# Fused transposes for the near strided blocks, a new opening order, and other units for the attention stages of two groups

## The chip, the cores and the metric

The kernel runs on one core of a Trainium2 chip. The metric is device time in microseconds (us), lower is better, as the median of several executions. One further execution is recorded by the hardware profiler; all trace times below are microseconds from the start of its span.

## The reference

Attention over 4 batches, 8 heads, 576 positions of 64 values. Heads 0 to 3 are local (a query sees the 32 positions up to itself), heads 4 to 7 strided (a query sees earlier positions with the same residue modulo 32). Its output feeds two feed-forward blocks.

```python
scores = np.where(masks, scale * q @ k.T, -1e9)
attn = exp(scores - max) / (sum + 1e-9);  x = attn @ v      # 2304 rows of 512
h = x @ w_in;  x = (h - tanh(h)) @ w_out                    # 512 -> 2048 -> 512
xn = x / rms(x) * rms_g
out = (silu(xn @ w_gate) * (xn @ w_val)) @ w_out2           # 512 -> 1536 -> 512
```

## The kernel before

The 2304 rows are cut into nine **blocks** of 256, numbered 0 to 8, and these into five **groups**: (0,1), (2,3), (4), (5,6), (7,8). The attention of a block gives one half of the tile `xs` (local heads) and the other half (strided heads). For each group the first feed-forward block runs over 16 **units** f: `pe_h` (12 matmuls into `ps_h`), tanh on ACT (L675), `dve_g` (`tg`, L680), a split into a high part on ACT (`g`, L686) and a low part on DVE (L691), and `pe_x` (12 or 24 matmuls into `ps_x`), which runs one or two units late. Every fp32 operand is split in two parts, hence three matmuls for each product. After group 4 the second feed-forward block follows, untouched by the change. A matmul of any kind has line 143, the helper `mm`.

**Attention in stages.** Blocks 0 to 3 are the near ones. A block's local heads (class `Local`, letter L) and, where the block is one run of positions, its strided heads (class `Dense`, letter D) go through stages with one letter each: `s` scores on PE into two PSUM banks; `m` row maximum on DVE (L289, or L292 for later blocks); `e` exponential on ACT (L303); `n` normalisation on DVE (`sm`, L313); `p` transposes on PE into a bank `ps_p` (L322); `c` copy to `pT` on ACT (L326); `v` the product with v on PE into `ps_v`; `y` the high part of the result on ACT (L329) and `z` its low part on DVE (L333), both into `xs`. Stages m, e, n, p, c, y, z each exist twice, for half 0 and half 1 (64 queries of two sub-blocks each). For a near D block a half is `sm` of 128 x 64 for each of four heads; `p` makes four transposes of 64 columns into 64 partitions for each half, and `v` contracts over 64 partitions.

**The opening.** Up to the third unit the order on all engines is written out by hand, in the text `START`. A word is a stage, a block, a kind, a half and a bank: `p0L1m0` is p of block 0, local, half 1, bank m0. `A`, `B`, `P`, `Q` with a number convert weight tile 0, 1, ... (scale on ACT, L162; merge on DVE, L168 and L169; high part on ACT, L176; low part on DVE, L180); `h`, `T`, `G`, `I`, `J`, `X` are the steps of the first three units. Each engine works through its own instructions in the order in which `START` names them. The loads are issued ahead of it, by the first line of `START`: table, q and k of blocks 0, v, then weights and block 1.

**After the opening** the stages of the next group's attention are spread over the units of the running group. `STINT` lists, for running groups 1, 2 and 3, the units f after whose `pe_h` a whole stage is put (a stage `s` carries m, e, n with it, `p` carries c, `v` carries y and z):

```python
def pe_work():
    if g in STINT:
        wk.run_pe(len(wk.pe) if f in STINT[g] else 0)
```

In group 2 the list works through v of block 5, then block 6: s, p of L, s of D, v of L, p, v of D. In group 3 it is s, p, v of block 7 and then of block 8. From group 1 on PE keeps program order; the other engines are ordered by a scheduler. Blocks 4, 5, 7 and 8 have their strided heads done without PE: GpSimd (POOL) multiplies (L495 for scores, L528 for values), DVE sums (L500, L535). Their v comes through the buffer `sv` (L476), which block 3's D uses before them, so that this load waits for v of block 3.

Of the kernel before, what the change touches and what calls it, by code (L numbers as in the profile page):

```python
# [7 lines left out]
F32 = mybir.dt.float32  # L8
# [14 lines left out]

START = """
<tabcdwABwCDwww2ww
W9 s0Lx m0L1 s0Dx e0L1 m0L0 e0L0 n0L1 p0L1m0 m0D0 m0D1 n0L0 e0D0 n0D0 c0L1a A0 p0L0h1 e0D1 p0D0m0 c0L0a s1Lx c0D0a
B0 s1Dx n0D1 P0 A1 m1L0 Q0 p0D1h0 v0Lm0 m1D0 e1L0 c0D1a y0L1 B1 y0L0 n1L0 v0Dh0 z0L0 m1L1 z0L1 e1D0 m1D1 y0D1 z0D1
y0D0 z0D0 e1L1 P1 p1L0m0 A2 e1D1 n1L1 h0h1 p1L1m1 c1L0a Q1 B2 n1D0 c1L1a h1h0 T0 P2 p1D0m0 T1 c1D0a n1D1 p1D1m1 G0
c1D1a v1Lh1 Q2 I0 G1 I1 y1L1 y1L0 v1Dm1 y1D1 y1D0 J0 J1 z1L1 A3 A4 z1L0 z1D1 z1D0 X0 B3 P3 B4 h2h1 T2 G2 I2 Q3 J2
"""  # L30


# [1 line left out]
def attn_moe_moe_kernel(  # L34
# [24 lines left out]
    nc = tc.nc  # L59
    B, _, NC, D = q_str.shape  # L60
# [41 lines left out]
    ps_h = ctx.enter_context(tc.tile_pool(name="ps_h", bufs=1, space=PSUM))  # L102
    ps_m = ctx.enter_context(tc.tile_pool(name="ps_m", bufs=1, space=PSUM))
# [11 lines left out]
    ident, mask, dmask = tab[:, 192:320], tab[:, 320:416], tab[:, 416:544]  # L115
# [128 lines left out]
    class Heads:  # L244
        def __init__(self, j):
            self.j, self.near, self.early = j, j < NEAR, j < EA
            self.ps, self.sm, self.nm, self.ss, self.pp, self.pT, self.v = {}, {}, {}, {}, {}, {}, {}
            self.slot = {}

        def room(self, name, i, words):  # L250

# [28 lines left out]
        def st_m(self, i):  # L280

            w, ps = self.w, self.ps
            self.sm[i] = sm = self.room("sm", i, 4 * w).rearrange("q (h p t) -> q h p t", h=2, p=2)
            self.nm[i] = nm = att.tile([128, 2, 2], F32, tag="nm", name="nm", bufs=4)
            self.ss[i] = att.tile([128, 2, 2], F32, tag="ss", name="ss", bufs=4)
            m = dmask if w == 128 else mask if not self.near else add[96][:, i] if w == 96 else add[64]
            for hh in range(2):
                if self.early:
                    nc.vector.tensor_reduce(out=nm[:, hh], in_=ps[hh][:, i], axis=AX.X, op=ALU.max)  # L289
                else:  # L290
                    for p in range(2):
# [23 lines left out]
            )  # L315

        def st_p(self, i, bank):
            self.pp[i] = ps = bank("ps_p")[0:self.w].rearrange("k (h p t) -> k h p t", h=2, p=2)
            sm = self.sm.pop(i)
            for hh in range(2):  # L320
                for p in range(2):
                    nc.tensor.transpose(ps[:, hh, p, :], sm[:, hh, p, :], ident)  # L322

        def st_c(self, i, copy):
            self.pT[i] = pT = self.room("pT", i, 512)[0:self.w].rearrange("k (h p t) -> k h p t", h=2, p=2)
            copy(out=pT, in_=self.pp.pop(i))  # L326

        def st_y(self, i):
# [10 lines left out]
    class Local(Heads):  # L339
        w = 96  # L340
# [73 lines left out]
    class Dense(Heads):  # L414
        def __init__(self, j, b, t0):
            super().__init__(j)
            self.b, self.w = b, 128 if t0 else 64
            self.at = [self.w * u for u in range(4)]

        def load_qk(self):  # L420
            w = self.w
# [11 lines left out]

        def load_v(self):
            t = wts.tile([128, 1024], F32, tag="w", name="dv") if self.early else one.tile([128, NC * D], F32, tag="sv", name="dv")
            t = t[0:self.w, :1024]
            self.v = t.rearrange("k (g f) -> k g f", g=4)
            nc.sync.dma_start(out=t, in_=(v_near if self.near else v_far)[self.b])

        def st_v(self, bank):  # L440
            ps = bank("ps_v").rearrange("r (i n g t) -> r i n g t", i=2, n=2, g=2)
            for i in range(2):
                pT = self.pT.pop(i)
                for g in range(2):
# [143 lines left out]
    class Work:  # L588
# [22 lines left out]
        @staticmethod  # L611
        def stage(o, nm):
            if nm == "s":
                o.st_s(bank_m)
                for i in range(2):
                    o.st_m(i)
                    o.st_e(i)
                for i in range(2):
                    o.st_n(i)
            elif nm == "p":  # L620
                for i in range(2):
                    o.st_p(i, bank_m)
                    o.st_c(i, nc.scalar.copy)
            else:
                o.st_v(bank_m)
                for i in range(2):
                    o.st_o(i)
            nxt = o.nxt
            if nxt:
                if nm == "s":  # L630
                    nxt.load_qk()
                if nm == "v" and isinstance(o, Local):
                    for i in range(2):
                        nxt.load_v(i)
                elif nm == "v":
                    nxt.load_v()
# [206 lines left out]
    xq, first_units, pg = [], units[:3], None  # L843
    del units[:3]

    def bank_of(tag):
        if tag == "x":
            return bank_x
        return lambda name: {"h": ps_h, "m": ps_m}[tag[0]].tile([128, 512], F32, tag=tag, name=name)

    def first(word):

        op, rest = word[0], word[1:]
        if op == "<":
            for c in rest:
                loads[c]()
        elif op == "W":
            z = att.tile([128, 512], F32, tag="sm", name="zero").bitcast(BF16)[:, :512]
            nc.vector.memset(z, 0.0)
            ps = bank_of("m0")("ps_w")  # L860
            for _ in range(int(rest)):
                mm(ps, z[:, :128], z, True, True)
        elif op in "ABPQ":
            w = st1.ws[int(rest)]
            pool, tag, e = st1.place(int(rest))
            if op == "A":
                w.scale()
            elif op == "B":
                w.merge()
                st1.i = int(rest) + 1  # L870
            elif op == "P":
                w.high(pool, tag)
            else:
                w.low(e)
        elif op == "h":
            pe_h(*first_units[int(rest[0])], bank_of(rest[1:]))
        elif op in "TGIJX":
            u = first_units[int(rest)]
            {"T": act_tanh, "G": dve_g, "I": g_hi, "J": g_lo, "X": pe_x}[op](*u)
            if op == "J":  # L880
                xq.append(u)
            if op == "X":
                xq.remove(u)
        else:
            j, kind, rest = int(rest[0]), rest[1], rest[2:]
            o = loc[j] if kind == "L" else strd[j][0]
            fn = getattr(o, "st_" + op)
            if op in "sv":
                fn(bank_of(rest))
            elif op == "p":  # L890
                fn(int(rest[0]), bank_of(rest[1:]))
            elif op == "c":
                fn(int(rest[0]), nc.scalar.copy)
            else:
                fn(int(rest))

# [98 lines left out]
def lay_out(inputs):  # L995
# [50 lines left out]
    def flat(*parts):  # L1046
        return _np.concatenate([a.reshape(*a.shape[:2], -1) for a in parts], axis=2)
# [5 lines left out]
    laid = dict(  # L1053
        near_l=flat(q_l[:, :, :8], k_l[:, :, :, :256]),
        near_v=flat(*(v_l[:, a:a + 96] for a in (0, 32, 96, 160))),
        near_d=flat(q_d[:, 0], keys(8)), v_near=values(8).reshape(B, 64, 1024),
        q_loc=q_l, k_loc=k_l, v_loc=v_l,
        q_str=lanes(q), k_str=lanes(k), v_str=lanes(v),
        q_far=q_d[:, 1], k_far=keys(16).reshape(B, 128, 1024), v_far=values(16).reshape(B, 128, 1024),
# [27 lines left out]
```

## Time and profile before

| | us |
|---|---|
| median of 3 runs | 929.55 (925.61 to 930.08) |
| the profiled execution, its own time | 927.72 |
| its span, first to last instruction | 925.9 |
| PE busy | 906.0 (98%) |
| DVE busy | 533.8 (58%) |
| ACT busy | 343.4 (37%) |
| POOL busy | 154.3 (17%) |

PE is the matmul engine, DVE VectorE, ACT ScalarE, POOL GpSimd, SP the queue that issues the loads. The span is nearly all PE time, so what matters is where PE stands still or runs at its lower clock, and what it is then waiting for.

### The profile page before, as it was taken

How to read it: one execution, taken by the hardware profiler on the slowest of the kernel's cores; microseconds unless marked ns; L12 is line 12 of the kernel's file. 1: busy time of each engine (PE TensorE's matmuls, PEld its weight loads, DVE VectorE, ACT ScalarE, POOL GpSimd, SP SyncE). 2: the span in 40 equal slices, each digit the busy share in tenths (PEclk: the TensorE clock that was granted, in tenths of full speed). 3: DMA queues.
4: the chain of work that ended last, by engine and by line, in shares of the span. 5: the costliest groups of instructions: out<-in, count | busy, mean ns of one | idle time of the engine just before them, and what ended most of it. 6: DMA issues, size and time to landing. Idle time of an engine off the chain costs nothing.

```text
span 925.9 us, 13596 instructions
## 1 busy us (share of the span) xinstructions
PE 906.0 (98%) x5251; PEld 754.7 (82%) x5251; DVE 533.8 (58%) x1195; ACT 343.4 (37%) x800; POOL 154.3 (17%) x211
## 2 busy tenths in 40 slices
PE   6999999998999999999999999999999999999998
PEld 4888878887898788888888888888888888888897
DVE  5899968986779886289996361272126212411221
ACT  5878633233443333366584131131122212211111
POOL 0000347782366852000000000000000000000000
PEclk8899999999999999999999999999999999999999
DMA  9946224220313100175462010110010001000100
GB/s 279 355 178 223 77 80 145 72 95 1 111 52 105 41 1 1 66 266 191 160 227 92 1 46 0 46 46 1 1 45 1 23 1 45 1 1 1 46 1 23
DMA packets 33729, 72.86 MB, mean 79 GB/s; under 512 B 6976, under 2 KB 15552, under 8 KB 33664
## 3 DMA queue, kind: packets, MB, share of 16 engines
q1 hardware_dynamic: 33664, 71.99, 23.3%
q8 instruction: 41, 0.67, 0.3%
q14 instruction: 24, 0.20, 0.1%
HBM read 62.54 MB, written 9.44 MB: 78 GB/s over the span
## 4 chain that ended last, share of the span: by engine, by line
PE 69%; DVE 5%; POOL 2%; ACT 1%; issue 0%; ACTq 0%; POOLq 0%; DVEq 0%
PE ps_x L143 26%; PE ps_h L143 26%; PE ps_m L143 16%; DVE so L535 3%; POOL pr L495 2%; DVE tg L680 1%; DVE g L691 0%; POOL pr L528 0%; PE ps_p L322 0%; ACT sm L303 0%; DVE sm L292 0%; PE ps_v L143 0%; DVE sm L313 0%; DVE xs L333 0%; DVE pr L543 0%
## 5 line engine op out<-in xcount | busy, mean ns | idle before, releaser
L143 PE MATMUL ps_h<-xs,w 128*128 128x512 f32 (+1 forms) x984 | 216.2, 369 | 3.9 <-DVE tg L680 3.9
L143 PE MATMUL ps_x<-g,w 128*128 128x512 f32 (+1 forms) x984 | 215.9, 368 | 0.0
L143 PEld LDWEIGHTS ps_h<-xs,w 128*128 128x128 f32 x984 | 171.1, 191 | 34.4 <-DVE tg L680 4.8
L143 PEld LDWEIGHTS ps_x<-g,w 128*128 128x128 f32 x984 | 169.5, 190 | 30.7 <-issue 0.2
L790 DVE SCALAR_TENSOR_TENSOR s<-ps_m,s 128x512 f32<-128x512 f32 (+1 forms) x60 | 38.3, 638 | 239.5 <-PE ps_m L143 239.5
L143 PE MATMUL ps_h<-xn,w 128*128 128x512 f32 (+1 forms) x720 | 158.9, 369 | 0.0
L143 PE MATMUL ps_m<-xn,w 128*128 128x512 f32 (+1 forms) x720 | 158.1, 368 | 0.0
L143 PE MATMUL ps_x<-w,p 128*128 128x512 f32 x648 | 157.8, 391 | 0.0
L143 PEld LDWEIGHTS ps_h<-xn,w 128*128 128x128 f32 x720 | 126.8, 188 | 24.4
L143 PEld LDWEIGHTS ps_m<-xn,w 128*128 128x128 f32 x720 | 125.9, 188 | 23.1
L143 PEld LDWEIGHTS ps_x<-w,p 128*128 128x128 f32 x648 | 120.7, 188 | 25.6
L495 POOL TENSOR_TENSOR pr<-sk,sq 128x256 f32<-128x256 f32 (+2 forms) x101 | 83.5, 862 | 132.7 <-DMA sk<-in_k_str_dram 107.3
L789 ACT ACTIVATE s<-ps_h 128x512 f32<-128x512 f32 (+1 forms) x60 | 33.4, 556 | 176.3 <-PE ps_h L143 176.1
L792 ACT CAST p<-s 128x512 fp32r<-128x512 f32 (+1 forms) x60 | 34.7, 578 | 128.7 <-DVE s L790 128.7
L528 POOL TENSOR_TENSOR pr<-sv,se 128x288 f32<-128x288 f32 (+12 forms) x104 | 70.4, 698 | 68.0 <-DVE so L535 19.6
L686 ACT CAST g<-tg 128x512 fp32r<-128x512 f32 (+1 forms) x82 | 46.4, 567 | 83.4 <-DVE tg L680 83.4
L675 ACT ACTIVATE tg<-ps_h 128x512 f32<-128x512 f32 (+1 forms) x82 | 44.4, 542 | 70.2 <-PE ps_h L143 70.0
L680 DVE SCALAR_TENSOR_TENSOR tg<-ps_h,tg 128x512 f32<-128x512 f32 (+1 forms) x82 | 50.7, 618 | 31.9 <-ACT tg L675 31.7
L535 DVE TENSOR_REDUCE so<-pr 128x16 f32<-128x272 f32 (+11 forms) x104 | 65.0, 650 | 5.3 <-POOL pr L528 5.0
L691 DVE TENSOR_TENSOR g<-tg,g 128x512 fp32r<-128x512 f32 (+1 forms) x82 | 56.3, 687 | 13.4 <-ACT g L686 12.8
L793 DVE TENSOR_TENSOR p<-s,p 128x512 fp32r<-128x512 f32 (+1 forms) x60 | 38.3, 638 | 27.5 <-ACT p L792 27.2
L162 ACT ACTIVATE ca<-raw 128x512 f32<-128x512 f32 x68 | 45.7, 673 | 19.4 <-DMA raw<-in_w_val_dram 7.1
(77 smaller groups left out, 621.4 us busy)
## 6 DMA issues: line engine op xcount, KB each, us to landing
raw<-in_w_out_dram SPq DMA_DIRECT2D x28, 512.0 KB, 5.1
raw<-in_w_in_dram SPq DMA_DIRECT2D x16, 512.0 KB, 8.5
raw<-in_w_gate_dram SPq DMA_DIRECT2D x12, 512.0 KB, 4.4
raw<-in_w_val_dram SPq DMA_DIRECT2D x12, 512.0 KB, 4.1
x2d<-xe SPq DMA_DIRECT2D x36, 128.0 KB, 1.8
x<-x2d SPq DMA_DIRECT2D x16, 256.0 KB, 4.3
out_dram<-o SPq DMA_DIRECT2D x16, 256.0 KB, 2.0
sk<-in_k_str_dram SPq DMA_DIRECT2D x4, 576.0 KB, 3.7
```

The costliest lines, as they stand in the source:

```text
L143: nc.tensor.matmul(out_, lhsT, rhs, start=start, stop=stop, skip_group_check=True)
L162: nc.scalar.activation(out=self.a, in_=hi.bitcast(F32), func=ACTF.Prelu, scale=2.0 ** -111, alpha=-(2.0 ** 32))
L495: nc.gpsimd.tensor_tensor(out=pr, in0=self.k[:, a:e, :], in1=self.q[:, c - c0:c - c0 + 1, :].to_broadcast([128, e - a, D]), op=ALU.mult,)
L528: nc.gpsimd.tensor_tensor(out=pr, in0=self.v[:, 0:c + 1, a:e], in1=self.e[:, c - c0, 0:c + 1].unsqueeze(2).to_broadcast([128, c + 1, e - a ...
L535: pend.append(lambda: nc.vector.tensor_reduce(out=o[:, c - g0, a:e], in_=pr.rearrange("l c d -> l d c"), axis=AX.X, op=ALU.add))
L675: nc.scalar.activation(out=t, in_=h_of[g, f, a], func=ACTF.Tanh, scale=WS)
L680: nc.vector.scalar_tensor_tensor(out=t, in0=h_of.pop((g, f, a)), scalar=WS, in1=t, op0=ALU.mult, op1=ALU.subtract)
L686: nc.scalar.copy(out=t[:, 0], in_=t_of[g, f, a])
L691: nc.vector.tensor_tensor(out=t[:, 1], in0=t_of.pop((g, f, a)), in1=t[:, 0].bitcast(F32), op=ALU.subtract)
L790: nc.vector.scalar_tensor_tensor(out=s, in0=r[1], scalar=WS, in1=s, op0=ALU.mult, op1=ALU.mult)
L792: nc.scalar.copy(out=t[:, 0], in_=s)
L793: nc.vector.tensor_tensor(out=t[:, 1], in0=s, in1=t[:, 0].bitcast(F32), op=ALU.subtract)
```

## The change

1. Near D blocks 0 to 3 (`fused`): both halves' `sm` lie side by side in one tile (half as the second last index), `p` makes four transposes of 128 columns instead of eight of 64, `c` one copy of 128 partitions instead of two of 64. `v` (`st_v2`) reads half i from partitions 64i to 64i+63 of `pT` and of v, which is laid out and loaded as 128 x 512 instead of 64 x 1024 (the same bytes), and writes the halves to two banks instead of one; the number of matmuls stays 32.
2. `START` is another text: same steps, another order.
3. `STINT`: in group 2 the first two stages stand after units 1 and 3 instead of 2 and 3; in group 3 the six stand after 1, 4, 6, 8, 11, 13 instead of 1, 3, 5, 8, 10, 12.

```diff
-W9 s0Lx m0L1 s0Dx e0L1 m0L0 e0L0 n0L1 p0L1m0 m0D0 m0D1 n0L0 e0D0 n0D0 c0L1a A0 p0L0h1 e0D1 p0D0m0 c0L0a s1Lx c0D0a
...
+W9 s0Lx m0L0 e0L0 m0L1 s0Dx n0L0 e0L1 m0D0 p0L0m1 m0D1 s1Lx A0 e0D0 B0 c0L0a n0L1 p0L1h1 P0 Q0 m1L0 m1L1 e0D1 c0L1a
+v0Lh0 s1Dx n0D1 n0D0 A1 e1L0 p0Dh1 e1L1 y0L1 n1L0 m1D0 m1D1 c0Da n1L1 v0Dm0m1 y0L0 e1D0 y0D1 z0L0 y0D0 z0L1 p1L0h1
...
-    STINT = {1: (4, 6, 8, 11, 14), 2: (2, 3, 6, 7, 9, 10, 13), 3: (1, 3, 5, 8, 10, 12)}
+    STINT = {1: (4, 6, 8, 11, 14), 2: (1, 3, 6, 7, 9, 10, 13), 3: (1, 4, 6, 8, 11, 13)}
...
         def st_p(self, i, bank):
-            self.pp[i] = ps = bank("ps_p")[0:self.w].rearrange("k (h p t) -> k h p t", h=2, p=2)
+            n = 2 * self.w if self.fused else self.w
+            self.pp[i] = ps = bank("ps_p")[0:n].rearrange("k (h p t) -> k h p t", h=2, p=2)
             sm = self.sm.pop(i)
             for hh in range(2):
                 for p in range(2):
-                    nc.tensor.transpose(ps[:, hh, p, :], sm[:, hh, p, :], ident)
+                    x = self.both[:, hh, p].rearrange("q i t -> q (i t)") if self.fused else sm[:, hh, p, :]
+                    nc.tensor.transpose(ps[:, hh, p, :], x, ident)
...
+        def st_v2(self, bank):
+            ps = [bank("ps_v")[:, :256].rearrange("r (n g t) -> r n g t", n=2, g=2) for _ in range(2)]
+            pT = self.pT.pop(0)
+            for g in range(2):
+                for n in range(2):
+                    for h in range(4):
+                        for i in range(2):
+                            a, r = 64 * h + 32 * n, slice(64 * i, 64 * i + 64)
+                            mm(
+                                ps[i][32 * h:32 * h + 32, n, g], self.v[r, g, a:a + 32],
+                                pT[r, h % 2, h // 2, 64 * g:64 * g + 64], True, True,
+                            )
```

How the instructions stand, at three places. ACT in the opening, before; `ca` is the scaling of a weight that has just been loaded (`raw_112` the first, `raw_118` the second), `sm` 128x64 the exponentials of D of block 0, `pT` the copies:

```order
L303 ACTIVATE sm_223,ss_225<-ps_s_182,nm_224 128x64 x2
L303 ACTIVATE sm_223,ss_225<-ps_s_183,nm_224 128x64 x2
L326 COPY pT_244<-ps_p_218 96x512
L162 ACTIVATE ca_246<-raw_112 128x512
L303 ACTIVATE sm_223,ss_230<-ps_s_182,nm_229 128x64 x2
L303 ACTIVATE sm_223,ss_230<-ps_s_183,nm_229 128x64 x2
L326 COPY pT_244<-ps_p_248 96x512
L326 COPY pT_283<-ps_p_257 64x512
L176 CAST w_311<-ct_285 128x512
L162 ACTIVATE ca_313<-raw_118 128x512
```

The same stretch of ACT in the change:

```order
L162 ACTIVATE ca_254<-raw_112 128x512
L310 ACTIVATE sm_218,ss_220<-ps_s_191,nm_219 128x64 x2
L310 ACTIVATE sm_218,ss_220<-ps_s_192,nm_219 128x64 x2
L336 COPY pT_263<-ps_p_224 96x512
L176 CAST w_273<-ct_260 128x512
L310 ACTIVATE sm_218,ss_230<-ps_s_191,nm_229 128x64 x2
L310 ACTIVATE sm_218,ss_230<-ps_s_192,nm_229 128x64 x2
L336 COPY pT_263<-ps_p_268 96x512
L162 ACTIVATE ca_335<-raw_118 128x512
```

The first weight's scaling has moved ahead of all exponentials of D, and no copy of D stands ahead of the second weight.

DVE in group 2, before: `xs<-ps_v` are the two z of block 5, `tg` those of units 1, 2 and 3, `so` sums of POOL's products:

```order
L680 SCALAR_TENSOR_TENSOR tg<-ps_h,tg 128x256
L535 TENSOR_REDUCE so<-pr 128x16 x2
L691 TENSOR_TENSOR g<-tg,g 128x256
L680 SCALAR_TENSOR_TENSOR tg<-ps_h,tg 128x256
L535 TENSOR_REDUCE so<-pr 128x16 x2
L691 TENSOR_TENSOR g<-tg,g 128x256
L535 TENSOR_REDUCE so<-pr 128x16
L333 TENSOR_TENSOR xs<-ps_v,xs 128x2x128
L543 STREAM_TRANSPOSE pr<-so 128x128
L333 TENSOR_TENSOR xs<-ps_v,xs 128x2x128
L554 TENSOR_TENSOR xs<-pr,xs 128x2x64
L680 SCALAR_TENSOR_TENSOR tg<-ps_h,tg 128x256
```

The same in the change:

```order
L708 SCALAR_TENSOR_TENSOR tg<-ps_h,tg 128x256
L563 TENSOR_REDUCE so<-pr 128x16 x2
L719 TENSOR_TENSOR g<-tg,g 128x256
L343 TENSOR_TENSOR xs<-ps_v,xs 128x2x128
L563 TENSOR_REDUCE so<-pr 128x16 x2
L343 TENSOR_TENSOR xs<-ps_v,xs 128x2x128
L563 TENSOR_REDUCE so<-pr 128x16
L708 SCALAR_TENSOR_TENSOR tg<-ps_h,tg 128x256
L571 STREAM_TRANSPOSE pr<-so 128x128
L719 TENSOR_TENSOR g<-tg,g 128x256
L582 TENSOR_TENSOR xs<-pr,xs 128x2x64
L708 SCALAR_TENSOR_TENSOR tg<-ps_h,tg 128x256
```

Both z have moved ahead of unit 2's `tg`, which in turn has moved behind them and three sums.

PE in group 3, before, from s of block 7 to the first matmuls after its p:

```order
L143 MATMUL ps_s<-lq 64x96 x16
L143 MATMUL ps_h<-xs,w 128x512 x12
L143 MATMUL ps_x<-g,w 128x512 x12
L143 MATMUL ps_h<-xs,w 128x512 x12
L322 MATMUL ps_p<-tab,sm 96x128 x8
L143 MATMUL ps_x<-g,w 128x512 x12
```

The same in the change:

```order
L143 MATMUL ps_s<-lq 64x96 x16
L143 MATMUL ps_h<-xs,w 128x512 x12
L143 MATMUL ps_x<-g,w 128x512 x12
L143 MATMUL ps_h<-xs,w 128x512 x12
L143 MATMUL ps_x<-g,w 128x512 x12
L143 MATMUL ps_h<-xs,w 128x512 x12
L331 MATMUL ps_p<-tab,sm 96x128 x8
L143 MATMUL ps_x<-g,w 128x512 x12
```

One x and one h of 12 matmuls now stand between s and p.

## Rows read from the trace of the kernel before

**Rows 1.** The page's first line: span and instructions.

```profile
span 925.9 us, 13596 instructions
```

**Rows 2.** Waits of PE, whole span: us in total, times, longest.

```profile
PE ps_h L143 <- DVE tg L680: 3.9, 2, 2.7
...
PE ps_p L322 <- DVE sm L313: 1.9, 1, 1.9
...
PE ps_s L143 <- DVE xs L333: 1.7, 1, 1.7
```

**Rows 3.** Windows of the opening: stretch, length, busy and count by engine, clock, DMA.

```profile
26.00:28.00 2.00, 1.80 (x9) 1.50 (x9) 1.74 (x5) 2.00 (x11) 0.00 (x0) 0.50 1.06 210
28.00:30.00 2.00, 1.94 (x16) 1.76 (x15) 1.76 (x8) 2.00 (x9) 0.00 (x0) 0.97 1.01 201
```

**Rows 4.** Timeline of ACT in the opening: start, us, what, [idle before, releaser].

```profile
10.14 0.21 ACT L303 ACTIVATION_READ_ACCUMULATOR sm<-ps_s,nm 128x1 f32 x1
...
12.91 0.68 ACT L162 ACTIVATE ca<-raw 128x512 f32<-128x512 f32 x1 [0.41 <-DMA raw<-in_w_in_dram]
...
14.65 1.06 ACT L326 COPY pT<-ps_p 96x512 f32<-96x512 f32 x2
...
18.66 0.70 ACT L162 ACTIVATE ca<-raw 128x512 f32<-128x512 f32 x1 [2.43 <-DMA raw<-in_w_in_dram]
...
20.52 0.57 ACT L326 COPY pT<-ps_p 64x512 f32<-64x512 f32 x1
```

**Rows 5.** Timeline of PE in the opening.

```profile
21.15 1.90 PE L143 MATMUL ps_v<-pT,dv 64*32 64x64 f32 x64 [1.64 <-ACT pT L326]
...
24.00 3.11 PE L143 MATMUL ps_h<-xs,w 128*128 128x256 f32 x12
...
28.02 1.71 PE L143 MATMUL ps_h<-xs,w 128*128 128x256 f32 x12
...
32.81 1.17 PE L143 MATMUL ps_v<-pT,dv 64*32 64x64 f32 x64
...
38.28 0.73 PE L143 MATMUL ps_h<-xs,w 128*128 128x512 f32 x2
40.23 3.99 PE L143 MATMUL ps_h<-xs,w 128*128 128x256 f32 x22 [1.21 <-DVE tg L680]
```

**Rows 6.** Timeline of DVE in the opening: the last z of block 0.

```profile
25.01 0.61 DVE L333 TENSOR_TENSOR xs<-ps_v,xs 128x256 fp32r<-128x256 f32 x1 [0.67 <-ACT xs L329]
```

**Rows 7.** Timelines of PE and of POOL: v of block 3, POOL's first value products.

```profile
123.98 0.69 PE L143 MATMUL ps_v<-pT,dv 64*32 64x64 f32 x32
...
129.00 5.22 POOL L528 TENSOR_TENSOR pr<-sv,se 128x272 f32<-128x272 f32 x8 [13.14 <-DMA sv<-in_v_str_dram]
```

**Rows 8.** Timeline of PE in groups 1 to 3: the three stalls.

```profile
214.71 4.54 PE L143 MATMUL ps_h<-xs,w 128*128 128x512 f32 x12 [2.69 <-DVE tg L680]
...
244.28 0.88 PE L143 MATMUL ps_s<-lq 64*64 64x96 f32 x30 [1.68 <-DVE xs L333]
...
301.90 2.89 PE L143 MATMUL ps_h<-xs,w 128*128 128x512 f32 x12
...
307.16 0.61 PE L322 MATMUL ps_p<-tab,sm 128*96 128x128 f32 x4 [1.93 <-DVE sm L313]
307.53 4.59 PE L143 MATMUL ps_x<-g,w 128*128 128x512 f32 x12
```

**Rows 9.** Timeline of DVE around the second stall: unit 1's low part, block 5's last z.

```profile
240.03 0.74 DVE L691 TENSOR_TENSOR g<-tg,g 128x256 fp32r<-128x256 f32 x1
...
243.71 0.42 DVE L333 TENSOR_TENSOR xs<-ps_v,xs 128x256 fp32r<-128x256 f32 x1 [0.22 <-ACT xs L329]
```

**Rows 10.** Timeline of PE: four 64-wide transposes, eight 128-wide ones.

```profile
71.90 0.60 PE L322 MATMUL ps_p<-tab,sm 128*64 128x128 f32 x4
...
268.69 1.36 PE L322 MATMUL ps_p<-tab,sm 128*128 128x128 f32 x8
```

**Rows 11.** Timeline of PE: scores of a D block on four tiles of 64 x 64.

```profile
103.76 0.69 PE L143 MATMUL ps_s<-dq 64*64 64x64 f32 x32
```

More of the change, by code (lines that the diff above doesn't have):

```diff
@@ L25 @@
 <tabcdwABwCDwww2ww
-W9 s0Lx m0L1 s0Dx e0L1 m0L0 e0L0 n0L1 p0L1m0 m0D0 m0D1 n0L0 e0D0 n0D0 c0L1a A0 p0L0h1 e0D1 p0D0m0 c0L0a s1Lx c0D0a
-B0 s1Dx n0D1 P0 A1 m1L0 Q0 p0D1h0 v0Lm0 m1D0 e1L0 c0D1a y0L1 B1 y0L0 n1L0 v0Dh0 z0L0 m1L1 z0L1 e1D0 m1D1 y0D1 z0D1
-y0D0 z0D0 e1L1 P1 p1L0m0 A2 e1D1 n1L1 h0h1 p1L1m1 c1L0a Q1 B2 n1D0 c1L1a h1h0 T0 P2 p1D0m0 T1 c1D0a n1D1 p1D1m1 G0
-c1D1a v1Lh1 Q2 I0 G1 I1 y1L1 y1L0 v1Dm1 y1D1 y1D0 J0 J1 z1L1 A3 A4 z1L0 z1D1 z1D0 X0 B3 P3 B4 h2h1 T2 G2 I2 Q3 J2
+W9 s0Lx m0L0 e0L0 m0L1 s0Dx n0L0 e0L1 m0D0 p0L0m1 m0D1 s1Lx A0 e0D0 B0 c0L0a n0L1 p0L1h1 P0 Q0 m1L0 m1L1 e0D1 c0L1a
+v0Lh0 s1Dx n0D1 n0D0 A1 e1L0 p0Dh1 e1L1 y0L1 n1L0 m1D0 m1D1 c0Da n1L1 v0Dm0m1 y0L0 e1D0 y0D1 z0L0 y0D0 z0L1 p1L0h1
+c1L0a B1 z0D0 P1 z0D1 p1L1h1 e1D1 c1L1a Q1 n1D0 n1D1 h0h0 A2 v1Lm1 T0 B2 A3 G0 y1L0 p1Dh1 c1Da y1L1 B3 v1Dh1m0 I0 P2
+J0 y1D1 z1L0 y1D0 h1h0 T1 z1L1 z1D1 z1D0 P3 h2h1 Q2 G1 A4 Q3 T2 B4 I1 G2 J1 I2 J2 X0
 """
@@ L247, in __init__ @@
             self.ps, self.sm, self.nm, self.ss, self.pp, self.pT, self.v = {}, {}, {}, {}, {}, {}, {}
-            self.slot = {}
+            self.slot, self.both, self.sums = {}, None, None
+            self.fused = False
         def room(self, name, i, words):
@@ L282, in st_m @@
             w, ps = self.w, self.ps
-            self.sm[i] = sm = self.room("sm", i, 4 * w).rearrange("q (h p t) -> q h p t", h=2, p=2)
+            if not self.fused:
+                sm = self.room("sm", i, 4 * w).rearrange("q (h p t) -> q h p t", h=2, p=2)
+            else:
+                if self.both is None:
+                    self.both = self.room("sm", 0, 8 * w).rearrange("q (h p i t) -> q h p i t", h=2, p=2, i=2)
+                sm = self.both[:, :, :, i]
+            self.sm[i] = sm
             self.nm[i] = nm = att.tile([128, 2, 2], F32, tag="nm", name="nm", bufs=4)
@@ L321, in st_p @@
                 for p in range(2):
-                    nc.tensor.transpose(ps[:, hh, p, :], sm[:, hh, p, :], ident)
+                    x = self.both[:, hh, p].rearrange("q i t -> q (i t)") if self.fused else sm[:, hh, p, :]
+                    nc.tensor.transpose(ps[:, hh, p, :], x, ident)
         def st_c(self, i, copy):
-            self.pT[i] = pT = self.room("pT", i, 512)[0:self.w].rearrange("k (h p t) -> k h p t", h=2, p=2)
+            n = 2 * self.w if self.fused else self.w
+            self.pT[i] = pT = self.room("pT", i, 512)[0:n].rearrange("k (h p t) -> k h p t", h=2, p=2)
             copy(out=pT, in_=self.pp.pop(i))
@@ L418, in __init__ @@
             self.at = [self.w * u for u in range(4)]
+            self.fused = self.near
         def load_qk(self):
@@ L435, in load_v @@
             t = wts.tile([128, 1024], F32, tag="w", name="dv") if self.early else one.tile([128, NC * D], F32, tag="sv", name="dv")
-            t = t[0:self.w, :1024]
-            self.v = t.rearrange("k (g f) -> k g f", g=4)
+            t = t[:, :512 if self.near else 1024]
+            self.v = t.rearrange("k (g f) -> k g f", f=256)
             nc.sync.dma_start(out=t, in_=(v_near if self.near else v_far)[self.b])
         def st_v(self, bank):
+            if self.near:
+                self.st_v2(bank)
+                return
             ps = bank("ps_v").rearrange("r (i n g t) -> r i n g t", i=2, n=2, g=2)
@@ L452, in st_v @@
             self.po = {i: ps[:, i].rearrange("r n g (l c) -> r n (g l) c", c=8) for i in range(2)}
+        def st_v2(self, bank):
[10 more added lines that the diff above has]
+                            )
+            self.po = {i: ps[i].rearrange("r n g (l c) -> r n (g l) c", c=8) for i in range(2)}
         def dst(self, i):
@@ L620, in stage @@
             elif nm == "p":
-                for i in range(2):
+                for i in range(1 if o.fused else 2):
                     o.st_p(i, bank_m)
@@ L844, in attn_moe_moe_kernel, with bank_of, bank @@
     del units[:3]
-    def bank_of(tag):
-        if tag == "x":
-            return bank_x
-        return lambda name: {"h": ps_h, "m": ps_m}[tag[0]].tile([128, 512], F32, tag=tag, name=name)
+    def bank_of(tags):
+        if tags == "x":
+            return bank_x
+        tags = [tags[k:k + 2] for k in range(0, len(tags), 2)]
+        def bank(name):
+            tag = tags.pop(0)
+            return {"h": ps_h, "m": ps_m}[tag[0]].tile([128, 512], F32, tag=tag, name=name)
+        return bank
     def first(word):
@@ L890, in first @@
             elif op == "p":
-                fn(int(rest[0]), bank_of(rest[1:]))
+                i = 0 if o.fused else int(rest[0])
+                fn(i, bank_of(rest if o.fused else rest[1:]))
             elif op == "c":
-                fn(int(rest[0]), nc.scalar.copy)
+                fn(0 if o.fused else int(rest[0]), nc.scalar.copy)
             else:
@@ L1055, in lay_out @@
         near_v=flat(*(v_l[:, a:a + 96] for a in (0, 32, 96, 160))),
-        near_d=flat(q_d[:, 0], keys(8)), v_near=values(8).reshape(B, 64, 1024),
+        near_d=flat(q_d[:, 0], keys(8)), v_near=values(8).reshape(B, 64, 2, 2, 256).transpose(0, 2, 1, 3, 4).reshape(B, 128, 512),
         q_loc=q_l, k_loc=k_l, v_loc=v_l,
```

## The prediction

> **What bounds the kernel now.** PE is busy for 906.0 of the span's 925.9 us [rows 1], so an edit counts only if it takes work from PE, shortens a wait of PE, or keeps PE off its lower clock. The waits of PE come first among the views: three of them lie behind the opening, 2.69 on `tg`, 1.93 on `sm`, 1.68 on `xs` (the two waits on `tg` sum to 3.9; the other, 1.21, ends the opening) [rows 2, 5, 8]. The windows come next, for the clock: it stands at 0.50 (1.2 of 2.4 GHz) in 26 to 28 us, where PE is busy for 1.80 of 2.00, and at 0.97 in the next window [rows 3]. What this costs stands in PE's timeline: twelve 256-wide matmuls take 3.11 before the rise and 1.71 after it, 1.40 more [rows 5]. Then the timeline around the three stalls: after those of 2.69 and 1.93, twelve 512-wide matmuls take 4.54 and 4.59, elsewhere 2.89 [rows 8]; each of these stalls thus costs some 1.7 more than it lasts. After that of 1.68 nothing is drawn out.
>
> The profiled execution took 927.72, 1.8 beyond its span and 1.83 below the median of 929.55; the sum is made against 927.72 and set against the median at the end.
>
> **Opening.** The order of ACT moves the first weight's scaling ahead of the exponentials of D. Those of L end at 10.35 (10.14 + 0.21) in both; the weight lands just ahead of 12.91 [rows 4], and no load moves, so ACT now stands idle for 2.6 us. The scaling and one set of exponentials then take 1.74 (12.91 to 14.65), and what follows is done before the second weight, at 18.66. That with a set of exponentials takes 1.86, to 20.52 [rows 4]; a further set, about 1.25 of it, ends at 21.8, a high part of L (estimate 0.3, half the 0.57 of the copy of twice its length) at 22.1, and the one copy of D, 0.57, at 22.65. Before, v of D started at 21.15 [rows 5]: the new order is 1.5 late here. v took 1.90 at the low clock and 1.17 at the full one [rows 5]; with 1.5, between these, it ends at 24.15. From its end to that of the last low part took 2.57 (21.15 + 1.90 to 25.01 + 0.61) [rows 5, 6], so h of the first unit starts at about 26.7 and ends, at 3.11, at 29.8; before, 24.00 + 3.11 = 27.1.
>
> This is regained behind it. Before, PE does h of the second unit and eight transposes and two copies of block 1's D ahead of v of that block, which ends at 33.98 [rows 5]. Now there stand between: v of L (about 1.15, as D's 1.17), four transposes 0.68, one copy 0.57, v of D 1.17: 33.4. Still to do are h of units two and three and x of the first, 1.71 each [rows 5], and 26 of the records of block 2's scores, 0.56 at the 0.69/32 of [rows 11]: 39.1. Before, the same set and two 512-wide matmuls (0.45) were followed by a stall of 1.21 to 40.23 [rows 5], which is 39.8 without the two. Now twelve matmuls into another bank come next, so that this `tg` has some 2 us of cover; without cover the 1.21 is back. Gain **0.7**. Bounds: 2.1 if h of the first unit runs at the full clock (1.40 more); a loss of 3.5 if the second, third and x all run at the low one (3 x 1.40 less 0.7).
>
> **Fused blocks.** Four 128-wide transposes cost 0.68 (half of 1.36), eight 64-wide ones 1.20 [rows 10]: 0.52 less for each near block at most, in the PE-bound stretch for blocks 2 and 3 only, as the opening has its own sum. There they are sown among 512-wide matmuls; I take 0.15 each, **0.3** in all, with 0 and 1.0 as bounds. The two banks instead of one, and halves that are read from other partitions, could slow or speed v. Its 64 records take 1.17, 18 ns each, on four tiles of 32 columns; D's scores take 0.69 for 32, 22 ns each, on four tiles of 64 x 64 that already use both halves of the rows [rows 5, 11]. Two kinds of tile at about one rate for each instruction: I take v as unchanged. Its bounds are half, 0.6 less for each of two blocks, and one of 1.90 instead of 1.17, 0.7 more for each.
>
> The Trainium skill, "TensorEngine Tiling (Array Packing)", section "Key Properties", says that different tiles run weight loads and matmuls in parallel; the new v uses eight tiles of 64 x 32 where four were used. By that rule v would halve, and the sum below would come out 1.2 lower; the trace speaks for the rate of instructions instead, in the two rows named.
>
> **First stall.** PE waits for a `tg` that stands on DVE behind block 4's sums of POOL's products, and POOL starts these when the load into `sv` lands, 4.3 us after v of block 3 (124.67 to 129.00) [rows 7]; from there POOL sets its own pace. v of block 3 comes 0.7 earlier for the opening, 0.3 for the transposes, and 0.7 for three 512-wide matmuls that now stand behind it (2.89/12 = 0.24 each): 1.7. PE arrives at the stall only 1.0 earlier, so it lasts 2.0 instead of 2.69, the half-clock matmuls stay, and what follows is **1.7** earlier. DVE's order there is the same.
>
> **Second stall.** PE's scores of block 6 wait until 244.28 for the last low part of block 5, which ends at 244.13 [rows 8, 9]. In the changed order v stands after unit 1, not 2, and both low parts ahead of unit 2's `tg`; they can follow unit 1's low part, which ends at 240.78 [rows 9], and three sums, by 242.5. PE asks at 242.6. Gain **1.5**, bounds 0 (high part on ACT as late as before) and 1.68. The late one is then `tg` of unit 2, behind three sums, but its h has a unit of matmuls ahead of its next reader.
>
> **Third stall.** p of block 7 waits for `sm`, ready at 307.16. It now comes one x and one h later, twelve 512-wide matmuls each, 5.8 us at 2.89, and the wait of 1.93 goes, and with it the half clock behind it (4.59 less 2.89 = 1.70) [rows 8]: **3.6**. Bounds: 1.9 if the clock falls later all the same, 3.8. PE reaches group 3 some 3.2 earlier than the others expect; the last stage there, v of block 8, also comes a unit later and keeps about two units before the next group needs it. For short waits on `tg` I give back **0.3** (0 to 1.9, one stall like this again).
>
> **Sum.** 1.7 + 1.5 + 3.6 - 0.3 = 6.5 (the opening and transposes are inside the 1.7). From 927.72 this is 921.2, from the median 923.05. The profiled run is one draw as the three are; I take the middle, **922**.
>
> **Rivals.**
> A, as summed: 922, its own range 919.5 to 925.
> B, the first stall no longer brings the low clock. It would last 2.0, close to the 1.93 that brought it and not far from the 1.68 that did not [rows 8]. 1.65 less (4.54 less 2.89), or 2.7 with a stall that also shrinks by a microsecond: 919 to 920.5. Against it: one row on either side.
> C, the opening pays nothing or costs: the idle time of ACT at 10.35 is certain, and if h of the second and third units stay at the low clock (1.40 each), the 0.7 turns into a loss of up to 2.1, and POOL's lead falls with it to nearly nothing: 924 to 927. For it: the rise came after a busy stretch of v, p and h [rows 3, 5], and the new order has gaps there.
> D, the change doesn't do what it says: group 3's stall moves to `tg` or to p of block 8, because DVE and POOL are what is late: 3.6 gone, 925 to 928. Against it: DVE is done with `sm` at 307.16 and PE comes 5.8 less 1.9 later than that.
> E, the other side: PE stays at the low clock from h of the first unit through the third unit's h and the first x (4.2) and through the next h and x of 512 columns (2 x 2.89 more, if halved throughout). 10 lost, against 5.1 gained in groups 2 and 3 by the two last stalls: 934.4. It decides from 5.1 lost, that is once the low clock outlasts x of the first unit and a 512-wide h of twelve (7.1). For it: gaps of PE at p, c and v of block 1; against it: before, PE rose after less than 5 us of such work.
>
> **How the numbers follow.** Chances: A 0.48, B 0.18, C 0.18, D 0.08, E 0.08. The range, 917.5 to 926.5, holds A and B, the bounds of v (1.2 below B) and most of C; D's upper half and E lie outside, with a little below. A change of 0.5% (4.6 us, 924.9) is about what a measurement can tell here. Faster by more: nine tenths of A, B, and little of C, 0.63. Slower by more: most of E, 0.06. The rest, 0.31, is within.
>
> **What the changed profile would show.** ACT idle from 10.35 to 12.9; h of the first unit ending near 29.8, not 27.1; no wait at 40 us; v of block 3 ending near 123.0 and POOL's values starting near 127.3; a stall of about 2.0 from 211.0 to 213.0 with 4.5 us behind it; none ahead of block 6's scores and none ahead of block 7's p; four transposes of 0.68 and v unchanged at 1.17. The prediction is wrong if the clock rises later than 30 us, if a wait of over 1.5 us appears in groups 3 or 4, or if the stall of group 1 changes by more than a microsecond.

## The result and the profile after

The changed kernel takes 917.12 us (median of 6) where the kernel before takes 929.05 beside it: ratio 0.986, interval 0.9833 to 0.9888, so 1.4% shorter and clear of the noise. One of the six executions ran at a granted clock of 0.556 and took 1495.84, and the ratio leaves it out. A later pair (e8 below) gave 914.42 and 928.29, ratio 0.9863 (0.9844 to 0.9881). The forecast was 922 with a range from 917.5: the sign was right, but the gain is 12 to 14 us, not 7, and the time lies just below the range. The profiled pair differs by 10.2 (925.9 and 915.7), and that is what the rows below account for.

The page's first line and the waits of PE behind the opening, of the kernel after (us in total, times, longest):

```profile
span 915.7 us, 13554 instructions
...
PE ps_h L143 <- DVE tg L708: 2.8, 2, 2.0
PE ps_p L331 <- DVE xs L343: 0.2, 1, 0.2
```

The waits of 1.7 on `xs` and 1.9 on `sm` [rows 2] are gone; the one on `tg` is now 2.0. ACT in the opening, the two scalings of weights, and PE's timeline there:

```profile
11.91 0.67 ACT L162 ACTIVATE ca<-raw 128x512 f32<-128x512 f32 x1 [1.39 <-DMA raw<-in_w_in_dram]
...
17.07 0.67 ACT L162 ACTIVATE ca<-raw 128x512 f32<-128x512 f32 x1 [0.67 <-DMA raw<-in_w_in_dram]
```

```profile
21.12 1.18 PE L143 MATMUL ps_v<-pT,dv 64*32 64x64 f32 x64 [0.78 <-ACT pT L336]
...
24.73 2.91 PE L143 MATMUL ps_h<-xs,w 128*128 128x256 f32 x12
...
30.29 0.86 PE L143 MATMUL ps_v<-pT,dv 64*32 64x64 f32 x64 [0.68 <-ACT pT L336]
31.07 1.70 PE L143 MATMUL ps_h<-xs,w 128*128 128x256 f32 x12
...
36.71 2.91 PE L143 MATMUL ps_h<-xs,w 128*128 128x512 f32 x12
```

Read beside [rows 4, 5]: the weights land 1.0 and 1.6 earlier than in the profile before, v of block 1 takes 0.86 instead of 1.17, no wait on `tg` follows, and the opening is over at 36.71. Before it was over at 39.78 (40.23 less the 0.45 of two 512-wide matmuls, the wait of 1.21 counted in). Then the timelines of PE and POOL further on, from the four transposes of a fused block:

```profile
72.49 0.60 PE L331 MATMUL ps_p<-tab,sm 128*128 128x128 f32 x4
...
117.45 0.86 PE L143 MATMUL ps_v<-pT,dv 64*32 64x64 f32 x64
...
122.37 5.63 POOL L556 TENSOR_TENSOR pr<-sv,se 128x272 f32<-128x272 f32 x8 [7.09 <-DMA sv<-in_v_str_dram]
...
208.80 4.61 PE L143 MATMUL ps_h<-xs,w 128*128 128x512 f32 x12 [2.03 <-DVE tg L708]
...
236.32 1.27 PE L143 MATMUL ps_s<-lq 64*64 64x96 f32 x32
...
302.55 1.04 PE L331 MATMUL ps_p<-tab,sm 128*96 128x128 f32 x8
...
342.08 3.05 PE L143 MATMUL ps_h<-xs,w 128*128 128x512 f32 x12 [0.72 <-DVE tg L708]
```

The lead over the profile before [rows 5, 7, 8] can be read off step by step: 3.1 at the end of the opening, 6.4 at the end of v of block 3 (118.31 against 124.67), 6.6 at POOL's first values, 5.9 at the release of the first stall, 8.0 at block 6's scores, whose stall is gone; block 7's p runs without a wait; a new wait of 0.7 at 342.08 gives a little back; 10.2 at the end.

### The profile page after: what moved, and what is told of

It is laid out like the page before. It is cut to its first block, busy times and chain, and to the rows that moved or that the text cites. A ratio compares the mean times of both kernels' runs of the same rounds, so it can differ in the third digit from the quotient of the medians.

```text
span 915.7 us, 13554 instructions
## 1 busy us (share of the span) xinstructions
PE 899.9 (98%) x5235; PEld 750.6 (82%) x5235; DVE 530.2 (58%) x1195; ACT 340.9 (37%) x796; POOL 153.1 (17%) x211
## 4 chain that ended last, share of the span: by engine, by line
PE 67%; DVE 5%; POOL 4%; issue 1%; ACT 1%; ACTq 0%; POOLq 0%; DVEq 0%
PE ps_x L143 25%; PE ps_h L143 25%; PE ps_m L143 16%; POOL pr L523 4%; DVE so L563 3%; POOL pr L556 1%; DVE tg L708 1%; DVE sm L299 0%; DVE g L719 0%; DVE sm L320 0%; ACT sm L310 0%; PE ps_p L331 0%; PE ps_v L143 0%; DVE sc L528 0%; DVE pr L571 0%
## 5 line engine op out<-in xcount | busy, mean ns | idle before, releaser
L528 DVE TENSOR_REDUCE sc<-pr 128x4 f32<-128x256 f32 (+2 forms) x101 | 44.2, 438 | 16.4 <-POOL pr L523 15.9
```

Of the source, the lines that this page charges most:

```text
L528: pend.append(lambda: nc.vector.tensor_reduce(out=s[:, c - c0, a:e], in_=pr, axis=AX.X, op=ALU.add))
```

## The experiments

e2, e7, e9 and e11 are built on the kernel before, the others on the changed kernel, with the edits shown. Ratios are to the kernel before, run beside them; span and times are those of one profile each. "Opening" is the time at which h of three units and x of the first are done. Where PE then waits on `tg` (before, e7, e9, e2, e11) the wait is counted in: it is the end of that wait less 0.45. "v3" is the end of v of block 3; then come the first stall and what the twelve matmuls behind it took.

| run | ratio, interval | span | opening | v3 | first stall, behind it |
|---|---|---|---|---|---|
| before | 1 | 925.9 | 39.78 | 124.67 | 2.69, 4.54 |
| e7_before_again | 0.9998 (0.9983 to 1.0012) | 923.2 | 38.59 | 123.47 | 2.68, 3.03 |
| e9_tile_order | 1.000 (0.9985 to 1.0015) | 923.8 | 39.03 | 123.59 | 3.25, 3.02 |
| e2_units_only | 0.9938 (0.9917 to 0.9959) | 921.7 | 39.91 | 126.32 | 2.68, 3.03 |
| e11_units_short_rows | 0.9949 (0.9930 to 0.9968) | 919.4 | 39.81 | 124.69 | 2.52, 3.03 |
| e5_unfused | 0.9924 (0.9904 to 0.9945) | 920.6 | 39.80 | 123.74 | 2.68, 4.27 |
| e12_unfused_short_rows | 0.9914 (0.9893 to 0.9935) | 915.8 | 35.70 | 119.63 | 2.55, 4.33 |
| e6_fused_old_order | 0.9867 (0.9849 to 0.9886) | 913.4 | 34.26 | 116.45 | 3.02, 4.57 |
| after | 0.986 (0.9833 to 0.9888) | 915.7 | 36.71 | 118.31 | 2.03, 4.61 |
| e8_after_again | 0.9863 (0.9844 to 0.9881) | 913.7 | 34.90 | 116.50 | 2.07, 4.61 |
| e1_old_units | 0.9899 (0.988 to 0.9918) | 917.1 | 34.78 | 116.39 | 2.55, 3.02 |
| e3_split_load | 0.9897 (0.9874 to 0.992) | 911.3 | 32.56 | 115.16 | 2.03, 3.02 |
| e4_half_order | 0.9849 (0.9827 to 0.9872) | 912.0 | 35.86 | 115.19 | none |
| e10_scores_earlier | 0.9858 (0.9836 to 0.988) | 911.6 | 34.41 | 116.02 | 1.28, 3.03 |

**The units.** e1 puts the old ones back into the changed kernel, e2 the new ones into the kernel before.

```diff
-    STINT = {1: (4, 6, 8, 11, 14), 2: (1, 3, 6, 7, 9, 10, 13), 3: (1, 4, 6, 8, 11, 13)}
+    STINT = {1: (4, 6, 8, 11, 14), 2: (2, 3, 6, 7, 9, 10, 13), 3: (1, 3, 5, 8, 10, 12)}
```

> The changed kernel with the old units for groups 2 and 3; all else as changed. Theory U (the moved units alone removed the second and third stall): both are back, about 1.7 ahead of block 6's scores and 1.9 ahead of block 7's p with half-clock matmuls (4.6) behind it, span 915.7 + 5 = about 921; the first stall stays near 2.0 and the release near 208.8. Rival: the earlier POOL chain and opening had already covered them; then no such stalls and a span within 1 us of 915.7.

> The kernel before with only the new units for groups 2 and 3. Theory U: the stalls of 1.68 and 1.93 go, the first stall stays at 2.7 with release at 214.7, span 925.9 - 5.2 = about 920.7. Rival: the units need the earlier opening; then one of the two stalls stays, in part or moved to another wait, and the span is 922.5 or more.

PE's timeline in e1:

```profile
235.41 0.88 PE L143 MATMUL ps_s<-lq 64*64 64x96 f32 x30 [1.69 <-DVE xs L343]
...
298.34 0.61 PE L331 MATMUL ps_p<-tab,sm 128*96 128x128 f32 x4 [1.98 <-DVE sm L320]
298.71 4.58 PE L143 MATMUL ps_x<-g,w 128*128 128x512 f32 x12
```

Both stalls are back as theory U says, the earlier opening notwithstanding; the span of 917.1 stays below the 921 expected: this opening was 1.9 shorter (34.78 against 36.71), and the matmuls behind the first stall took 3.02 instead of 4.61. In e2 both are gone, and the ratio gives 5.8. Against e8, the changed kernel again, e1 costs 0.36%, 3.3 us, with intervals that just touch.

**Order of the opening, and fusing.** e5 keeps the new order and takes the near strided heads from the kernel before (transposes, copies, v and its load); e6 keeps them fused and takes the old order.

```diff
-... p0Dh1 ... c0Da ... v0Dm0m1 ... p1Dh1 c1Da ... v1Dh1m0
+... p0D0h1 p0D1m0 ... c0D0a c0D1a ... v0Dm1 ... p1D0h1 p1D1m0 c1D0a c1D1a ... v1Dh1
```

```diff
 (old START)
-... p0D0m0 ... c0D0a ... p0D1h0 ... c0D1a ... v0Dh0 ... p1D0m0 ... c1D0a ... p1D1m1 ... c1D1a ... v1Dm1
+... p0Dh0 ... c0Da ... v0Dh0m1 ... p1Dm1 ... c1Da ... v1Dm1m0
```

> The changed kernel with its order of the opening and its units, but the near strided heads as before: eight transposes of 64 columns, two copies, v over 64 partitions into one bank, v loaded as 64 rows of 4 KB. Theory S (the order of the opening gives most of what the opening gained): x of the first unit ends at 36 to 38.5, v of a block takes 1.17, v of block 3 ends 2.0 to 3.0 later than in the changed kernel (each near block costs 0.3 more in v and 0.5 in transposes), span some 2 to 3 above that of the changed kernel, 917.5 to 919. Theory F (fusing gives the opening its gain): x of the first unit ends at 39 or later and the span is 920 or more.

> The changed kernel with the opening in the order of before (four words less, since transposes and copies are fused). Theory S: x of the first unit ends near 39 with a wait on tg of about 1 behind it, as in the kernel before and in the run of the units alone; fusing saves only in group 0, so the span is 1.5 to 2.5 below the 921.7 of the units alone, near 919.5. Theory F: x of the first unit ends at 37 or earlier and the span is within 1.5 of 915.7.

Theory S fell, and theory F holds. With the old order and fused blocks (e6) the opening ends at 34.26, and the ratio is that of the change; the span, 913.4, is 2.3 below 915.7, where at most 1.5 was expected. e2 and e6 differ by the fused blocks and their load alone: 0.9938 and 0.9867, apart by 0.7%, 6.6 us, with intervals that do not meet. e5 and e8 (the change) differ by the same: 0.9924 and 0.9863, 5.7 us, and do not meet either. The ratios carry this; the opening of one profile would not, since e12 below, unfused like e5 and in the same order, opened at 35.70. From the opening to v3 the fused blocks give 2.7 in the old order (84.9 in before and e7, 82.2 in e6) and 2.3 in the new one (83.9 in e5, 81.6 in after and e8). What is left of 6.6 and 5.7, some 3.4 to 3.9, is an estimate of the opening's part.

In e5, e2 and e9 PE also stands still for 1.1 to 1.3 within v of block 0, with no wait in the profile that would explain it; in e6, e7, e10 and e12 it is 0.2 to 0.4. Its cause stays open, and so does its part in the late openings of e5 and e2.

**The same kernels again.** e7 and e8 are before and after, unchanged.

> The kernel before, unchanged, for a second profile. Theory V (where the first loads land and whether the low clock follows a stall varies from one execution to the next): the first weight lands between 10.4 and 13.4, not at 12.91, the twelve matmuls behind the first stall take either 3.0 or 4.5, and the end of the opening stays near 40. Rival: both are fixed by the kernel; then 12.9, 18.7 and 4.5 come again within 0.3.

> The changed kernel, unchanged, for a second profile. Theory V: landings of the first two weights differ from 11.9 and 17.1 by up to 2, and x of the first unit ends between 32.6 and 38 with them; the matmuls behind the first stall take 3.0 or 4.6; span 911 to 917. Rival: landings at 11.9 and 17.1, x of the first unit at 36.7 and 4.6 behind the stall again, span within 0.5 of 915.7.

Theory V holds. The first two weights are scaled at 12.46 and 15.65 in e7 (12.91 and 18.66 before), at 10.94 and 15.27 in e8 (11.91 and 17.07). With the same stall of 2.68, the matmuls behind it took 3.03 in e7, not 4.54. In both e7 and e8 no row shows ACT waiting for a landing there, so the weights may have landed earlier still. e7 is also the fair partner of e6 up to v3, with nearly the same start of the second weight's scaling (15.65 and 15.47); that e6 has the new units matters only later. PE in e7 and then in e6, from v of block 0 on:

```profile
20.64 0.85 PE L143 MATMUL ps_v<-pT,dv 64*32 64x64 f32 x36 [0.36 <-issue]
...
26.51 1.67 PE L143 MATMUL ps_h<-xs,w 128*128 128x256 f32 x12
28.63 0.60 PE L322 MATMUL ps_p<-tab,sm 128*64 128x128 f32 x4 [0.45 <-DVE ss L311]
29.38 0.60 PE L322 MATMUL ps_p<-tab,sm 128*64 128x128 f32 x4 [0.15 <-DVE sm L313]
...
31.64 1.17 PE L143 MATMUL ps_v<-pT,dv 64*32 64x64 f32 x64
...
39.04 3.98 PE L143 MATMUL ps_h<-xs,w 128*128 128x256 f32 x22 [1.21 <-DVE tg L680]
```

```profile
19.12 0.46 PE L143 MATMUL ps_v<-pT,dv 64*32 64x64 f32 x32 [0.18 <-issue]
...
24.71 2.06 PE L143 MATMUL ps_h<-xs,w 128*128 128x256 f32 x12
26.97 0.63 PE L331 MATMUL ps_p<-tab,sm 128*128 128x128 f32 x4 [0.20 <-DVE sm L320]
...
28.61 0.86 PE L143 MATMUL ps_v<-pT,dv 64*32 64x64 f32 x64
...
34.26 4.86 PE L143 MATMUL ps_h<-xs,w 128*128 128x512 f32 x24
```

v of block 0 ends 1.9 earlier in e6 (19.58 against 21.49). From the end of h of the second unit to the end of v of block 1 it is 2.7 instead of 4.6: one set of transposes, one copy, a shorter v, and none of block 2's scores between (12 records in e7). The wait of 1.21 is gone; all five profiles with unfused blocks in the old order have it (1.21 or 1.22). The opening is 4.3 shorter, though h of the first two units ran at a lower clock in e6 (2.06 against 1.67 for the second). From there to v3 it is 82.2 instead of 84.9.

**The load of v.** In the first two profiles the loads of 8 to 10 us moved 180 GB/s before and 305 after. e3 splits the fused load over the partitions, e12 (on e5) and e11 (on e2) give the unfused one rows of 2 KB instead of 4.

```diff
 (e3)
-            nc.sync.dma_start(out=t, in_=v_near[self.b])
+            for r in (slice(0, 64), slice(64, 128)):
+                nc.sync.dma_start(out=t[r], in_=v_near[self.b][r])
 (e11, e12)
+            for c in (slice(0, 512), slice(512, 1024)):
+                nc.sync.dma_start(out=t[:, c], in_=v_near[self.b][:, c])
```

> The changed kernel, but the near strided heads' v is loaded by two transfers, one for each half of the partitions, rows of 2 KB as in the change. Theory P (transfers onto 64 partitions move at half the rate, as 180 GB/s in 8 to 10 us of the kernel before): the first weight lands near 12.9 and the second near 18.7 again, h of the first unit starts 1.0 to 1.6 later than 24.73, span 917 to 919. Theory R (it is the length of the rows, 4 KB before, 2 KB now): landings stay at 11.9 and 17.1 and the span within 0.7 of 915.7.

> The run with unfused blocks and the new order, but v of the near strided heads is loaded by two transfers with rows of 2 KB instead of one with rows of 4 KB, onto the same 64 partitions. Theory R (rows of 4 KB load slowly, and the weights queued behind them land later): the first weight lands at 10.4 to 11.9 instead of 12.6, the second at 14.8 to 17.1 instead of 17.9, x of the first unit ends 1.0 to 2.5 earlier than 39.9, span 1 to 2.5 below 920.6. Rival (fusing shortens the chain of transposes, copies and v, and landings scatter anyway): landings as in the other unfused runs, x of the first unit at 39 or later, span within 1 of 920.6.

> The kernel before with the new units and with v of the near strided heads loaded by two transfers with rows of 2 KB instead of one with rows of 4 KB; opening in the old order, blocks not fused. Theory R (the rows of the load make a good part of what fusing gives): 8 to 11 us of the load move at over 330 GB/s, the second weight's scaling starts by 16.0, x of the first unit and what goes with it ends 1 to 3 earlier than the 39 to 39.9 of the unfused runs, the median 1 to 4 below the 921.6 of the units alone. Rival (it is the chain of transposes, copies and v): the opening ends at 38.5 or later and the median is within 1 of 921.6.

The second weight's scaling in e12 and then in e11:

```profile
15.73 0.68 ACT L162 ACTIVATE ca<-raw 128x512 f32<-128x512 f32 x1 [0.24 <-DMA raw<-in_w_in_dram]
```

```profile
18.80 0.70 ACT L162 ACTIVATE ca<-raw 128x512 f32<-128x512 f32 x1 [2.16 <-DMA raw<-in_w_in_dram]
```

The profile of e3 speaks against theory P: two loads onto 64 partitions each were as quick (342 GB/s in 5 to 11 us, second weight at 14.84) as one. Its time does not settle it: 0.9897 is 0.34% above the 0.9863 of e8, with intervals that overlap a little. e12 looked like theory R, e11 contradicts it: same rows of 2 KB, 252 GB/s and 18.80. In time neither differs from its partner (0.9914 and 0.9924; 0.9949 and 0.9938). The loads scatter from one execution to the next, by 219 to 319 GB/s in 5 to 11 us in the five profiles with one load onto 64 partitions (mean 273), and by 282 to 370 in the six with one onto 128 (mean 337). Whether that shape shifts the mean stays open, and with it how much of the gain of fusing is the load's.

**v.** e4 runs half 0 and then half 1 through the fused v; e9 swaps two loops in v of the kernel before, so that neighbours go to different tiles.

```diff
 (e4)
-            for g in range(2):
-                for n in range(2):
-                    for h in range(4):
-                        for i in range(2):
+            for i in range(2):
+                for g in range(2):
+                    for n in range(2):
+                        for h in range(4):
 (e9)
-                    for h in range(4):
-                        for n in range(2):
+                    for n in range(2):
+                        for h in range(4):
```

> The changed kernel, but v does all matmuls of half 0 first and then those of half 1, so that neighbours use the same rows. Theory Q (neighbours on different halves of the rows overlap): v takes 1.17 again instead of 0.86 in the stretch at full clock and 1.9 instead of 1.2 in the opening; v of block 3 ends 1.0 to 1.6 later than 118.3, span 916.5 to 918. Rival (two banks or the new layout make it faster): v stays at 0.86 and the span within 0.4 of 915.7.

> The kernel before with one edit: in v of the near strided heads the loop over heads is the inner one, so that neighbours go to different tiles of 32 columns, as in the change; before, each tile gets two in a row. One bank and 64 partitions as before. Theory N (two in a row for the same tile wait for each other): v takes 0.99, as in the run of halves in sequence, instead of 1.17; v of block 3 ends 0.4 to 0.6 earlier, the span 0.5 to 1 below the 923.2 to 925.9 of the kernel before. Rival (two banks give it): v stays at 1.17.

PE in e4 and in e9:

```profile
114.20 0.99 PE L143 MATMUL ps_v<-pT,dv 64*32 64x64 f32 x64
```

```profile
77.60 1.10 PE L143 MATMUL ps_v<-pT,dv 64*32 64x64 f32 x64
```

Both theories were half right: 1.17 before, 1.10 with the loops swapped, 0.99 with two banks and both halves of the partitions one after the other, 0.86 with the halves taking turns. The step from 1.10 to 0.99 comes with a second bank and with the other half of the partitions; which of the two makes it was not separated. e4 has a side effect: v of block 3 comes 79.3 after the opening instead of 81.6, that much earlier in PE's work, and the first stall is gone; so its total says nothing about v.

**The first stall.** e10 moves the scores of block 5.

```diff
-    STINT = {1: (4, 6, 8, 11, 14), ...
+    STINT = {1: (4, 6, 8, 10, 14), ...
```

> The changed kernel with one number changed: in group 1 the scores of block 5 stand after unit 10 instead of 11, so that their maxima and normalisation leave DVE before the last sums of block 4. Theory D (the first stall is DVE's queue of these and the sums): the stall of 2.0 falls below 0.5 and with it any half-clock matmuls, span 910 to 913.5. Rival (POOL's chain sets it): the stall stays at 2.0 and the span within 1 of 913.7 to 915.7.

```profile
199.24 3.01 PE L143 MATMUL ps_h<-xs,w 128*128 128x512 f32 x12 [0.23 <-DVE tg L708]
...
206.26 3.03 PE L143 MATMUL ps_h<-xs,w 128*128 128x512 f32 x12 [1.28 <-DVE tg L708]
```

DVE just ahead of the `tg` that ends the second of these waits:

```profile
204.93 0.68 DVE L563 TENSOR_REDUCE so<-pr 128x21 f32<-128x252 f32 x1 [0.23 <-POOL pr L556]
```

Theory D does not hold: 2.03 becomes 1.28 and 0.23, not less than 0.5. The release hardly moves, 90.2 after v3 where it is 90.5 in after and 90.4 in e8, and DVE now stands idle until POOL's products come. That speaks for the rival, POOL's chain; the wait is shorter mainly because PE comes half a microsecond later to it (89.0 after v3 instead of 88.5). Neither e4 nor e10 can be told from the change by its interval; no version was found that is surely better.

## Why the prediction was wrong, step by step

None of the three signs of being wrong that it named came: the granted clock was back at 0.93 in 28 to 30 us, no wait in groups 3 and 4 was over 0.7, and the first stall changed by 0.7. The miss lay where it had set no sign.

**Opening, 0.7 forecast, 3.1 in the profiled pair and 4.3 between e7 and e6: the step that failed.** Three parts of the walk were wrong. First, "no load moves, so ACT now stands idle for 2.6 us": the landings were taken from one profile as fixed. But the second weight's scaling starts at 18.66 and 15.65 in two profiles of the same kernel, and anywhere from 14.84 to 18.80 in all fourteen. In the changed kernel's profile ACT waited 1.39, and v started at 21.12, where the walk had 22.65. The chain itself held: from that scaling to v 4.05 (17.07 to 21.12), forecast 3.99, and from the end of h of the first unit to the end of the opening 9.1, forecast 9.3. Of the 2.4 by which the walk ended late (39.1 against 36.71), 1.6 is the landing. An earlier start of that scaling isn't worth the same in both kernels either: after, e8 and e1 end the opening 19.6 behind it, so it is passed on in full (the other fused runs, each with an edit of its own, lie at 17.7 to 19.1), while the kernel before passed on 1.2 of 3.0 (39.78 to 38.59). Second, the walk looked for gain and loss in the new order; e6 shows the same total with the old order. The order is worth nothing measurable with fused blocks; without them the ratios differ by 0.14% (e5 and e2) and 0.35% (e12 and e11), with intervals that overlap. Third, the fused stages were counted only by their own transposes. In the opening p, c and v of two blocks stand one after the other on the path to h and x, and with each of them shorter the wait on `tg` is gone too, in e6 even in the old order.

**v unchanged: wrong.** The row of D's scores was read as a rate of instructions that v could not beat; v takes 0.86, 13 ns for a record instead of 18. The comparison with the scores misled: they are another kind of tile, and the old v gave each tile two matmuls in a row, which alone makes 1.17 instead of 1.10 (e9). The Trainium skill, "TensorEngine Tiling (Array Packing)", "Key Properties", says that different tiles run in parallel; the trace agrees in direction, with 0.86, not with the 0.59 of a full halving.

**Transposes, 0.3: too small.** Four of 128 columns take 0.60 in the stream, as four of 64 do [rows 10], not the 0.68 of half a row of eight. Both rows name the same 128x128 operand, and differ only in the other, `128*128` and `128*64`. The way from the opening to v3 shrank by 3.3 (84.9 to 81.6). Taking PE's rows from each start to the next, the transposes of D in it went from 1.60 to 0.72 and v of D from 2.65 to 1.57: together 2.0 for the two blocks, and e5 with 4.16 and e6 with 2.28 confirm this as the share of fusing. The three matmuls that now stand behind v of block 3 make 0.8, the transposes and v of L 0.5 (mostly there in e5 too, so not from fusing), and the rest cancels.

**First stall: mechanism right, size follows the opening.** v3, the load, POOL and the release move together: 6.4, 6.6 and 5.9, where 1.7 was forecast. PE's wait is 2.03 for a forecast 2.0, and not by luck: PE comes to it 5.2 earlier (206.77 against 212.02), 0.7 less than the release, as the walk had it.

**Second and third stalls: right.** Both went with the units, for 1.5 and 3.6 forecast; at block 6's scores the lead grew from 5.9 to 8.0. At the end it is 10.2, or 10.9 with what was given back, so 2.9 for the third. By the ratios the units are worth 5.8 (e2) and 3.3 (e1). **Given back:** 0.3 forecast, a wait of 0.7 seen.

**Low clock behind a stall: the rule was wrong.** Rival B rested on the length of the wait. Stalls of 2.03 were followed by 4.61 (after, granted clock 0.59 in 208.8 to 211 us) and by 3.02 (e3, clock 1.00 in 206 to 209), and one of 3.25 by 3.02 (e9). Behind the third stall it is the same: 4.58 behind 1.98 in e1, 2.98 behind 2.04 in e9. So the 1.7 is a matter of the execution, not of a length between 1.68 and 1.93, and the part of it in the 3.6 for the third stall is a draw as well.

## What to carry to other kernels

Before a walk through an opening is trusted to a microsecond, profile the same kernel twice: what repeats is the chain, what doesn't is where loads land and where the clock falls. Price a merged stage by the chain on which it stands, with the waits behind it, and not by its instructions alone; and test the parts of a change crosswise (each alone, each left out), since here the part on which the walk spent most of its steps, the new order, gave least.

## What was not expected of the hardware

The granted clock differs between executions of one program: mean over 12 to 28 us 0.61 in the profile before and 0.81 in e7, 0.50 after and 0.68 in e8. A 64 x 32 matmul's pace depends on the matmuls beside it and on the banks: 1.17, 1.10, 0.99 and 0.86 for the same 64 records in the kernel before, e9, e4 and the change.
